# Reordering the first masks, first outputs and last stores of a Mamba-2 SSD plus squared-ReLU MoE kernel

## The chip, the core and the metric

The kernel runs on one core of a Trainium2 chip. The metric is the device time in microseconds of one execution. The time of the kernel before is the median of eight executions, 115.31 us (114.85 to 115.7).

The core's engines work side by side and meet through semaphores: TensorE (PE in the profile, its weight loads PEld), VectorE (DVE), ScalarE (ACT), GpSimd (POOL) and SyncE (SP), which only issues transfers here. GpSimd issues the transfers that turn float32 weights into bfloat16 on their way.

## The reference

A scan in chunks (Mamba-2's SSD form) is followed by a feed-forward layer with a squared ReLU. Cut to what matters:

```python
# x: [4, 8, 768, 32], a: [4, 8, 768], B and C: [4, 8, 768, 16]; chunks of 32
for c in range(nc):
    L = exp(cum_i - cum_j) * (i >= j)            # cum: cumulative sum of log a in the chunk
    y = ((C @ B.T) * L) @ x                       # within the chunk
    y += (C @ state) * exp(cum)                   # from the state
    state = exp(sum(log a)) * state + sum_j decay_from_j * outer(B_j, x_j)
h = maximum(y.reshape(3072, 256) @ w_in, 0)       # w_in: 256 x 2048
out = (h * h) @ w_out                             # w_out: 2048 x 256, out: 3072 x 256 float32
```

The kernel does the same with chunks of 256 tokens: the decays are folded into B and C as cumulative products, so that the scores need only a mask of zeros and ones.

## The kernel before, in words

There are 12 units, one for each of 4 batches and 3 stretches of 256 tokens (`UNITS`, line 124). A unit goes through these steps:

- `ph_load` brings C, B and x; `prep_c` and `prep_b` scale C and B and write them in bfloat16 into a tile `jt`; `ph_tr` transposes that tile into `bct` (on TensorE for units 0 to 4, with a copy back from PSUM).
- `ph_mt` makes the scores in the four PSUM banks 0 to 3. `ph_mask(k, q)` multiplies bank q with the mask into `mts`. Where `ph_raw(k, q)` ran before, ScalarE has copied the bank to SBUF as bfloat16 first, and the mask is applied to that copy.
- `ph_yu(y=, u=)` makes the outputs of unit y (`within`: `mts` with x; `from_state`: the state `Sd` with C) and the state products of unit u. The outputs are copied from PSUM into `T[y]`.
- `ph_s(k, i)` builds the next state `z` and its spread form `Sd`, for which it needs `QP`, a table of decays. Lists such as `later` hold back the second half of that.
- `mm1(blk, fp)` multiplies T with two columns of blocks of w_in and ends in a ReLU on ScalarE (`hb`), `square` squares it on VectorE (`h`), `mm2` multiplies with w_out and adds up over eight values of fp. After the last, the result is copied to `osb` and stored.

The order of all instructions is written out by hand: each engine runs its own in the order in which the Python code calls them. For the first 16 MoE steps that order is the list `first` (line 558), afterwards the loop at line 613. Everything that the change touches at the start lies in lines 478 to 511, between the transposes of unit 0 and the first `u00` of that list. There:

- `prep_c(1)`, the table QP (line 478), `load_w_out(0)` and `load_w_in(2)` are GpSimd's, in one queue with its computing.
- Unit 0's masks q = 0, 1, 3, 2 are VectorE's, with `prep_b(1)` and the first `Sd` (line 493) between the first and the second.
- `idle_products` are matmuls without use that keep TensorE busy; `NIDLE` (line 50) gives their number and width.
- `ph_mt(1)`, then `ph_yu(u=1)`, `ph_s(1, 0)` and `ph_yu(y=0, ...)` follow on TensorE.
- GpSimd then issues the further weights and unit 2's C, B and x.

w_in is loaded in five tiles (`W_TILES`); tile 2 holds the columns for fp 2 and 3. At the end, `mm2` runs `LAG` = 4 steps behind `mm1`, so five of its calls stand after the last `mm1`. The last unit's two halves of 128 tokens (r = 0 and 1) go to two PSUM banks and are stored by SyncE and ScalarE.

Of the kernel before, what the change touches and what calls it, by code (L numbers as in the profile page):

```python
# [10 lines left out]
FP32 = mybir.dt.float32  # L11
# [12 lines left out]
def _dap(base: bass.AP, offset_elems: int, dims):  # L24

    return bass.AP(tensor=base.tensor, offset=base.offset + offset_elems,
                   ap=[list(d) for d in dims])
# [3 lines left out]
def kernel(  # L31
# [13 lines left out]
    nc = tc.nc  # L45
    NH, S, D, N = 8, 768, 32, 16
    NU = 12
    LAG = 4
    NPE = 5
    NIDLE = ((7, 512), (2, 128), (4, 256), (2, 256), (4, 256), (3, 128), (3, 256))  # L50

    const = ctx.enter_context(tc.tile_pool(name="const", bufs=1))
    wpool = ctx.enter_context(tc.tile_pool(name="w", bufs=1))
# [7 lines left out]
    opool = ctx.enter_context(tc.tile_pool(name="opool", bufs=2))  # L61
# [91 lines left out]
    def load_w_in(i):  # L153
        f, n = W_TILES[i]
        nc.gpsimd.dma_start(out=w_in_b[i], in_=_dap(moe_w_in, f, [[2048, 128], [128 * 2048, 2], [1, 128 * n]]))  # L155

    def load_w_out(i):
        n = 4 if i else 2
        nc.gpsimd.dma_start(out=w_out_b[i], in_=_dap(
            moe_w_out, i * 512 * 256, [[256 * n, 128], [256 * 256, 4 // n], [1, 256 * n]]))  # L160
# [6 lines left out]
    def prep_c(k, eng):  # L167
        b, j = UNITS[k]
        for g in range(2):
            eng.tensor_tensor(  # L170
                out=_fap(jt[k % 3], 128 + 144 * g, [[384, 2], [32, 4], [1, 16]]),
                in0=_fap(loaded[k]["C"], 128 * g, [[16, 2], [32, 4], [1, 16]]),
                in1=_fap(P_sb, b * 24 + 12 * g + j, [[96, 2], [3, 4], [0, 16]]), op=ALU.mult)

    def prep_b(k, eng):
        b, j = UNITS[k]
        for g in range(2):
            o = _fap(jt[k % 3], 16 * g, [[384, 2], [32, 4], [1, 16]])
            i = _fap(loaded[k]["B"], 128 * g, [[16, 2], [32, 4], [1, 16]])
            if k == 0:  # L180
                eng.copy(out=o, in_=i)
            else:
                eng.tensor_tensor(out=o, in0=i, in1=_fap(Pinv, b * 24 + 12 * g + j, [[96, 2], [3, 4], [0, 16]]),  # L183
                                  op=ALU.mult)
# [64 lines left out]
    def ph_mt(k, qs=range(4)):  # L249
        v = live[k]  # L250
        bct = v["bct"]
        for r in range(2):
            for u in range(2):
                for q in qs:
                    nc.tensor.matmul(  # L255
                        pp[64 * u:64 * u + 64, q, r * 256:r * 256 + 256],
                        bct[32 * q:32 * q + 32, r, 0, u * 64:u * 64 + 64],
                        _fap(bct[32 * q:32 * q + 32], 128 + u * 64, [[128, 2], [384, 2], [1, 64]]),
                        start=True, stop=True, skip_group_check=True,
                        tile_position=(32 * q, 64 * u))  # L260
        if "mts" not in v:
            v["mts"] = big.tile([128, 4, 2, 2, 128], BF16, tag="mts", name=f"mts{k}")
# [3 lines left out]
    def ph_raw(k, q):  # L266
        t = prep.tile([128, 512], BF16, tag="raw", name=f"raw{k}_{q}")
        nc.scalar.copy(out=t, in_=pp[:, q, :])
        raw_scores[(k, q)] = t

    def ph_mask(k, q):
        t = raw_scores.pop((k, q), None)
        nc.vector.tensor_tensor(  # L273
            out=live[k]["mts"][:, q],
            in0=(pp[:, q, :] if t is None else t).rearrange("p (r g i) -> p r g i", r=2, g=2),
            in1=_fap(mask, 0, [[128, 2], [0, 2], [1, 128]]), op=ALU.mult)
# [74 lines left out]
    def ph_s(k, i, later=None, raw=None, eng=None):  # L351

        b, j = UNITS[k]
        v = live[k]
        if i == 0:
            v["S"] = [state.get(b, (None, None, None))[2]]
        if j == 2 and i == 1:
            return
        z_old, p_old, _ = state.get(b, (None, None, None))
        h, c = v["U"][i]  # L360
        held.discard(h)
        z = spool.tile([128, 64], FP32, tag=f"z{b}", name=f"z{k}_{i}")
        u_in = pp[:, h, c:c + 64] if raw is None else raw
        if z_old is None:
            nc.scalar.copy(out=z, in_=pp[:, h, c:c + 64])
        else:
            nc.vector.scalar_tensor_tensor(out=z, in0=z_old, scalar=p_old, in1=u_in,  # L367
                                           op0=ALU.mult, op1=ALU.add)
        S_d = spool.tile([128, 256], BF16, tag=f"Sd{b}{i}", name=f"Sd{k}_{i}")

        def on_pool():
            (eng or nc.gpsimd).tensor_tensor(  # L372
                out=_fap(S_d, 0, [[128, 2], [32, 4], [1, 32]]),
                in0=_fap(z, 0, [[32, 2], [0, 4], [1, 32]]),
                in1=_fap(QP, ((b * 3 + j) * 2 + i) * 4, [[0, 2], [1, 4], [0, 32]]), op=ALU.mult)

        if later is None:
            on_pool()
        else:
            later.append(on_pool)  # L380
        state[b] = (z, Ptot[:, i, b * 3 + j:b * 3 + j + 1], S_d)
        v["S"].append(S_d)
# [18 lines left out]
        nc.vector.tensor_tensor(out=h2, in0=hb, in1=hb, op=ALU.mult)  # L401
        h2s[(blk, fp)] = h2

    def mm2(blk, fp):
        h2 = h2s.pop((blk, fp))
        end = blk == NU - 1
        for r, i in [(r, i) for r in range(2) for i in range(2)] if end else [(r, i) for i in range(2) for r in range(2)]:
            f = 2 * fp + i
            o = pp[:, r, 0:256] if end else pp[:, 7 if blk else 6, r * 256:(r + 1) * 256]
            nc.tensor.matmul(o, h2[:, i, r * 128:(r + 1) * 128], w_out_b[f // 4][:, f % 4, :],  # L410
                             start=(f == 0 and (end or r == 0)), stop=(f == 15), skip_group_check=True)
        if fp < 7:
            return
        b, j = UNITS[blk]
        o = (b * S + j * 256) * 256
        osb = opool.tile([128, 512], FP32, tag="osb", name=f"osb{blk}")
        if end:
            nc.vector.tensor_copy(out=osb[:, 0:256], in_=pp[:, 0, 0:256])
            nc.scalar.copy(out=osb[:, 256:512], in_=pp[:, 1, 0:256])
            for r, eng in enumerate((nc.sync, nc.scalar)):  # L420
                eng.dma_start(out=_dap(out, o + r * 256, [[512, 128], [1, 256]]), in_=osb[:, r * 256:(r + 1) * 256])
        else:
            nc.scalar.copy(out=osb, in_=pp[:, 7 if blk else 6, :])  # L423
            nc.sync.dma_start(out=_dap(out, o, [[512, 128], [1, 512]]), in_=osb)

    with tc.manual_schedule():
# [37 lines left out]
        for r in range(2):  # L464
# [10 lines left out]
        pps = pp[:, hp, 256:280].rearrange("p (u c) -> p u c", u=2)  # L475
        nc.tensor.matmul(pps, spread, pick_p, start=True, stop=True)
        nc.scalar.copy(out=Ptot, in_=pps)
        nc.gpsimd.tensor_tensor(
            out=_fap(QP, 0, [[8, 12], [4, 2], [1, 4]]), in0=_fap(Ptot, 0, [[1, 12], [12, 2], [0, 4]]),
            in1=_fap(quad, 0, [[0, 12], [0, 2], [1, 4]]), op=ALU.mult)  # L480
        prep_c(1, nc.gpsimd)
        load_w_out(0)
        load_w_in(2)
        idle_products(*NIDLE[3])
        later = []
        ph_mt(0)
# [2 lines left out]
        ph_yu(u=0)  # L489
        U01 = const.tile([128, 64], FP32, name="U01")  # L490
        nc.scalar.copy(out=U01, in_=pp[:, 7, 384:448])
        prep_b(1, nc.vector)
        ph_s(0, 0, eng=nc.vector)
        ph_raw(0, 2)
        idle_products(*NIDLE[4])
        ph_tr(1)
        idle_products(*NIDLE[6])
        for q in (1, 3, 2):
            ph_mask(0, q)
        xs = prep.tile([128, NH, 2 * D], BF16, tag="xs", name="xs1")  # L500
        nc.scalar.copy(out=xs, in_=loaded[1]["x"])  # L501
        live[1]["xs"] = xs
        ph_mt(1)
        ph_yu(u=1)
        ph_s(1, 0)
        load_w_out(1)
        load_w_in(3)
        ph_yu(y=0, late=True, h=(4, 5))
        ph_raw(1, 3)
        for q in range(4):  # L510
            ph_mask(1, q)
        ph_load(2, "CB", nc.gpsimd)
        load_w_out(2)
        load_x(2)
# [94 lines left out]
        for k in range(6, NU):  # L609
            at({6: 23, 7: 31, 8: 36}.get(k, 8 * k - 33), ph_load, k)  # L610
            at({6: 28, 7: 33}.get(k, 8 * k - 25), ph_prep, k)
            at({6: 31}.get(k, 8 * k - 20), ph_tr, k)
        for s in range(16, len(ups) + LAG):
            for fn, args, kw in todo.pop(s, []):
                fn(*args, **kw)
            if s < len(ups):
                mm1(*ups[s], any(fn is ph_yu for fn, _, _ in todo.get(s + 1, [])))
            if 17 <= s <= len(ups):
                square(*ups[s - 1])
            if s == 16:  # L620
                mm2(1, 7)
            elif 19 <= s < 26:
                mm2(*ups[s - 3])
            elif s > 26:
                mm2(*ups[s - LAG])
# [1 line left out]
_INS = ['x', 'a', 'B', 'C', 'moe_w_in', 'moe_w_out']  # L627
_OUTS = [((3072, 256), 'float32')]
# [25 lines left out]
```

## Time and profile before

| what | value |
|---|---|
| median of eight executions | 115.31 us (114.85 to 115.7) |
| the profiled execution, its time | 114.85 us |
| its span in the profile | 113.1 us |
| TensorE busy | 107.3 us, 95% of the span |
| VectorE busy | 81.5 us, 72% |
| ScalarE busy | 75.5 us, 67% |
| GpSimd busy | 47.7 us, 42% |
| granted TensorE clock | full in every slice of the span |
| transfers | 13.18 MB, 117 GB/s on average |

A line of the timeline gives start, length, engine, source line, operation, output from input, the shape with types, and how many instructions it merges; in brackets stands how long the engine had been idle and what ended that. The chain of waits is followed back from the last instruction: at each step to what released it, or to the instruction before it on its engine. "Landing" is the time from a transfer's issue to its arrival. Engines overlap successive instructions a little, so that the next may start some 0.1 us before the one ahead of it ends.

How the time of TensorE divides over the span, by stretches:

| stretch, us | TensorE busy | VectorE | ScalarE | GpSimd |
|---|---|---|---|---|
| 6 to 9 | 2.75 | 2.87 | 2.14 | 2.98 |
| 9 to 12 | 1.92 | 3.00 | 2.30 | 1.86 |
| 12 to 15 | 2.85 | 1.99 | 1.96 | 3.00 |
| 15 to 24 | 9.00 | 7.02 | 5.46 | 3.02 |
| 24 to 100 | 75.99 | 58.87 | 55.07 | 33.29 |
| 100 to 113 | 9.88 | 4.73 | 6.60 | 0.00 |

### The profile page before, as it was taken

What the parts mean: (1) busy time and instruction counts of PE and PEld (TensorE: products, weight loads), DVE (VectorE), ACT (ScalarE), POOL (GpSimd) and SP (SyncE); (2) the same over time, 40 slices, a digit from 0 to 9 for tenths busy, and PEclk for the clock granted to TensorE, in tenths of its full rate; (3) what the DMA queues carried; (4) which work ended last, traced back from release to release, by engine and by line L of the source; (5) the groups of instructions that cost most, each with busy time, mean ns of one, the idle gap of its engine ahead of it and who ended that gap; (6) DMA issues with size and microseconds to landing.
All of it is one profiled execution on the core that took longest, in us unless ns stands there. A gap on an engine that the chain in (4) does not pass through costs nothing.

```text
span 113.1 us, 3923 instructions
## 1 busy us (share of the span) xinstructions
PE 107.3 (95%) x1603; PEld 91.8 (81%) x1603; DVE 81.5 (72%) x186; ACT 75.5 (67%) x139; POOL 47.7 (42%) x98
## 2 busy tenths in 40 slices
PE   6997899999999999999999999999999999999980
PEld 2454699888878989989989889899899899899960
DVE  4499868697797999869679777578488487354440
ACT  3367776637886777777776767767766767877830
POOL 6495991146996496390578065074020020000000
PEclk9999999999999999999999999999999999999999
DMA  3999999989895674926999928441050020200202
GB/s 63 205 173 152 167 215 177 165 152 168 151 276 59 105 196 87 171 97 112 195 215 116 160 100 151 102 139 29 6 148 17 22 80 3 71 28 0 93 0 93
DMA packets 45250, 13.18 MB, mean 117 GB/s; under 512 B 41392, under 2 KB 43376, under 8 KB 45232
## 3 DMA queue, kind: packets, MB, share of 16 engines
q1 hardware_dynamic: 40736, 10.13, 46.3%
q0 software_dynamic: 3200, 2.49, 14.9%
q10 hardware_dynamic: 1296, 0.32, 1.3%
q8 instruction: 12, 0.20, 0.9%
q14 instruction: 6, 0.05, 0.2%
HBM read 10.64 MB, written 3.15 MB: 122 GB/s over the span
## 4 chain that ended last, share of the span: by engine, by line
PE 92%; ACT 3%; DVE 1%; issue 1%
PE pp L391 38%; PE pp L410 38%; PE pp L288 7%; PE pp L164 4%; PE pp L255 3%; PE pp L240 1%; ACT bct L232 1%; DVE xs L190 1%; ACT hb L395 1%; ACT T L348 1%; PE pp L465 0%; ACT xs L501 0%; PE pp L217 0%; PE pp L231 0%; DVE h L401 0%
## 5 line engine op out<-in xcount | busy, mean ns | idle before, releaser
L395 ACT ACTIVATE hb<-pp 128x512 bf16<-128x512 f32 x96 | 56.5, 597 | 25.3 <-PE pp L391 22.8
L391 PE MATMUL pp<-T,w_in_b 128*128 128x256 bf16 x384 | 56.6, 273 | 0.7 <-ACT T L348 0.7
L410 PE MATMUL pp<-w_out_b,h 128*128 128x256 bf16 x384 | 56.5, 273 | 0.1
L401 DVE TENSOR_TENSOR h<-hb 128x512 bf16<-128x512 bf16 x96 | 43.1, 457 | 18.1 <-ACT hb L395 17.9
L391 PEld LDWEIGHTS <-w_in_b 128*128 128x128 bf16 x384 | 40.2, 110 | 4.6 <-issue 2.8
L410 PEld LDWEIGHTS <-h 128*128 128x128 bf16 x384 | 37.2, 98 | 4.3 <-DVE h L401 0.5
L273 DVE TENSOR_TENSOR mts<-pp,mask 128x512 bf16<-128x512 f32 x45 | 30.4, 682 | 0.3 <-PE pp L255 0.2
L372 POOL TENSOR_TENSOR Sd<-z,QP 128x256 bf16<-128x256 f32 x19 | 12.0, 643 | 27.9 <-DVE z L367 24.9
L170 POOL TENSOR_TENSOR jt<-C_nat,P_sb 128x128 bf16<-128x128 f32 x20 | 9.3, 484 | 6.7 <-DMA C_nat<-in_C_dram 6.2
L183 POOL TENSOR_TENSOR jt<-B_nat,Pinv 128x128 bf16<-128x128 f32 x18 | 8.3, 483 | 1.3 <-DMA B_nat<-in_B_dram 0.7
L367 DVE SCALAR_TENSOR_TENSOR z<-z,Ptot,pp 128x64 f32<-128x64 f32 x14 | 3.9, 279 | 5.4 <-ACT T L348 4.9
L164 PE MATMUL pp<-idle 128*128 128x256 bf16 (+2 forms) x25 | 6.2, 393 | 1.1 <-DVE idle L439 1.1
L348 ACT CAST T<-pp 128x512 bf16<-128x512 f32 x10 | 5.9, 586 | 1.3 <-PE pp L288 0.8
L423 ACT COPY osb<-pp 128x512 f32<-128x512 f32 x11 | 6.4, 582 | 0.2 <-PE pp L410 0.2
L195 POOL CAST xs<-x_nat 128x512 bf16<-128x512 f32 x9 | 6.2, 685 | 0.9 <-DMA x_nat<-in_x_dram 0.7
L255 PE MATMUL pp<-bct 32*64 32x256 bf16 x192 | 5.1, 280 | 0.4 <-ACT bct L232 0.3
L164 PEld LDWEIGHTS <-idle 128*128 128x128 bf16 x25 | 2.8, 125 | 3.2 <-issue 1.9
L288 PE MATMUL pp<-mts,xs 64*32 64x128 bf16 x352 | 5.3, 219 | 0.0
L288 PE MATMUL pp<-bct,Sd 128*128 128x128 bf16 x40 | 4.2, 220 | 0.0
L288 PEld LDWEIGHTS <-xs 64*32 64x32 bf16 x352 | 3.7, 90 | 0.4 <-issue 0.2
L155 POOL DMA_DIRECT2D w_in_b<-in_moe_w_in_dram x5 | 3.8, 762 | 0.3 <-issue 0.3
L288 PEld LDWEIGHTS <-Sd 128*128 128x128 bf16 x40 | 3.1, 98 | 0.4
(69 smaller groups left out, 44.4 us busy)
## 6 DMA issues: line engine op xcount, KB each, us to landing
x_nat<-in_x_dram SPq DMA_DIRECT2D x11, 256.0 KB, 4.1
out_dram<-osb SPq DMA_DIRECT2D x11, 256.0 KB, 3.4
C_nat<-in_C_dram SPq DMA_DIRECT2D x11, 128.0 KB, 3.4
B_nat<-in_B_dram SPq DMA_DIRECT2D x9, 128.0 KB, 3.6
w_out_b<-in_moe_w_out_dram POOLq DMA_DIRECT2D x4, 256.0 KB, 5.0
w_in_b<-in_moe_w_in_dram POOLq DMA_DIRECT2D x3, 256.0 KB, 6.0
w_in_b<-in_moe_w_in_dram POOLq DMA_DIRECT2D x2, 128.0 KB, 3.9
B_nat<-in_B_dram ACTq DMA_DIRECT2D x1, 128.0 KB, 3.3
```

Source lines behind the costliest of these rows:

```text
L164: nc.tensor.matmul(pp[:, 5, 0:cols], idle, _fap(idle, 0, [[0, cols // 128], [1, 128]]), start=True, stop=True, skip_group_check=True)
L170: eng.tensor_tensor(out=_fap(jt[k % 3], 128 + 144 * g, [[384, 2], [32, 4], [1, 16]]), in0=_fap(loaded[k]["C"], 128 * g, [[16, 2], [32, 4], ...
L183: eng.tensor_tensor(out=o, in0=i, in1=_fap(Pinv, b * 24 + 12 * g + j, [[96, 2], [3, 4], [0, 16]]), op=ALU.mult)
L255: nc.tensor.matmul(pp[64 * u:64 * u + 64, q, r * 256:r * 256 + 256], bct[32 * q:32 * q + 32, r, 0, u * 64:u * 64 + 64], _fap(bct[32 * q:32 ...
L273: nc.vector.tensor_tensor(out=live[k]["mts"][:, q], in0=(pp[:, q, :] if t is None else t).rearrange("p (r g i) -> p r g i", r=2, g=2), in1 ...
L288: nc.tensor.matmul(dst, w, v, start=bool(need), stop=False, skip_group_check=True, **({} if pos is None else {"tile_position": pos}))
L348: nc.scalar.copy(out=_fap(T[y], 0, [[64, 2], [128, 4], [1, 64]]), in_=_fap(pp, h[0] * 512, [[(h[1] - h[0]) * 512, 2], [64, 4], [1, 64]]))
L372: (eng or nc.gpsimd).tensor_tensor(out=_fap(S_d, 0, [[128, 2], [32, 4], [1, 32]]), in0=_fap(z, 0, [[32, 2], [0, 4], [1, 32]]), in1=_fap(QP ...
L391: nc.tensor.matmul(pp[:, h, i * 256:(i + 1) * 256], _fap(w_in_b[wb], g * 128 * n + f, [[n, 128]]), T[blk][:, g].rearrange("p r u t -> p (r ...
L395: nc.scalar.activation(out=hb.rearrange("p i t -> p (i t)"), in_=pp[:, h, :], func=AF.Relu)
L401: nc.vector.tensor_tensor(out=h2, in0=hb, in1=hb, op=ALU.mult)
L410: nc.tensor.matmul(o, h2[:, i, r * 128:(r + 1) * 128], w_out_b[f // 4][:, f % 4, :], start=(f == 0 and (end or r == 0)), stop=(f == 15), s ...
```

## The change

At the start:

- GpSimd prepares C of unit 1 and issues `load_w_out(0)` before it builds QP.
- On VectorE, mask (0, 1) comes right after mask (0, 0), ahead of `prep_b(1)`; then masks (0, 3) and (0, 2), and the first `Sd` after all of them.
- `load_w_in(2)` is issued behind a copy of one element of `mts` to `spare`, which waits for mask (0, 2).
- After `ph_mt(1)`, ScalarE copies bank 0 (before: bank 3, later), and GpSimd applies mask (1, 0) to that copy; VectorE applies (1, 1), (1, 2), (1, 3) from PSUM, and then makes unit 1's first `Sd`, which GpSimd made before.
- Unit 0's outputs come ahead of unit 1's state products on TensorE.
- Two of the idle products' numbers change: one of 128 columns less, one of 256 more.

At the end: the last unit's last four fp are worked off by halves in an order written out, so that half 0 is complete four matmuls before the end; each half has a staging tile, a copy and a store of its own.

```diff
-    NIDLE = ((7, 512), (2, 128), (4, 256), (2, 256), (4, 256), (3, 128), (3, 256))
+    NIDLE = ((7, 512), (2, 128), (4, 256), (2, 256), (4, 256), (2, 128), (4, 256))
...
-    def ph_mask(k, q):
+    def ph_mask(k, q, eng=None):
         t = raw_scores.pop((k, q), None)
-        nc.vector.tensor_tensor(
+        (eng or nc.vector).tensor_tensor(
...
-    def mm2(blk, fp):
-        h2 = h2s.pop((blk, fp))
+    def mm2(blk, fp, rs=(0, 1)):
+        h2 = h2s[(blk, fp)]
         end = blk == NU - 1
-        for r, i in [(r, i) for r in range(2) for i in range(2)] if end else [(r, i) for i in range(2) for r in range(2)]:
+        for r, i in [(r, i) for r in rs for i in range(2)] if end else [(r, i) for i in range(2) for r in range(2)]:
...
-        osb = opool.tile([128, 512], FP32, tag="osb", name=f"osb{blk}")
+        osb = opool.tile([128, 512], FP32, tag="osb", name=f"osb{blk}_{rs[0]}")
         if end:
-            nc.vector.tensor_copy(out=osb[:, 0:256], in_=pp[:, 0, 0:256])
-            nc.scalar.copy(out=osb[:, 256:512], in_=pp[:, 1, 0:256])
-            for r, eng in enumerate((nc.sync, nc.scalar)):
-                eng.dma_start(out=_dap(out, o + r * 256, [[512, 128], [1, 256]]), in_=osb[:, r * 256:(r + 1) * 256])
+            r = rs[0]
+            (nc.scalar.copy if r else nc.vector.tensor_copy)(out=osb[:, 0:256], in_=pp[:, r, 0:256])
+            (nc.scalar if r else nc.sync).dma_start(
+                out=_dap(out, o + r * 256, [[512, 128], [1, 256]]), in_=osb[:, 0:256])
...
         nc.scalar.copy(out=Ptot, in_=pps)
+        prep_c(1, nc.gpsimd)
+        load_w_out(0)
         nc.gpsimd.tensor_tensor(
             out=_fap(QP, 0, [[8, 12], [4, 2], [1, 4]]), in0=_fap(Ptot, 0, [[1, 12], [12, 2], [0, 4]]),
             in1=_fap(quad, 0, [[0, 12], [0, 2], [1, 4]]), op=ALU.mult)
-        prep_c(1, nc.gpsimd)
-        load_w_out(0)
-        load_w_in(2)
...
+        first_state = []
+        ph_s(0, 0, later=first_state, eng=nc.vector)
+        ph_mask(0, 1)
         prep_b(1, nc.vector)
-        ph_s(0, 0, eng=nc.vector)
         ph_raw(0, 2)
         idle_products(*NIDLE[4])
         ph_tr(1)
         idle_products(*NIDLE[6])
-        for q in (1, 3, 2):
+        for q in (3, 2):
             ph_mask(0, q)
+        for fn in first_state:
+            fn()
+        nc.gpsimd.tensor_copy(out=spare, in_=live[0]["mts"][:, 2, 0, 0, 0:1])
+        load_w_in(2)
...
         ph_mt(1)
+        ph_raw(1, 0)
+        ph_mask(1, 0, nc.gpsimd)
+        ph_yu(y=0, late=True, h=(4, 5))
         ph_yu(u=1)
-        ph_s(1, 0)
+        second_state = []
+        ph_s(1, 0, later=second_state, eng=nc.vector)
         load_w_out(1)
         load_w_in(3)
-        ph_yu(y=0, late=True, h=(4, 5))
-        ph_raw(1, 3)
-        for q in range(4):
+        for q in (1, 2, 3):
             ph_mask(1, q)
+        for fn in second_state:
+            fn()
...
-        for s in range(16, len(ups) + LAG):
+        for s in range(16, len(ups) + 1):
...
-            elif s > 26:
+            elif 26 < s < len(ups):
                 mm2(*ups[s - LAG])
+        for fp, r in ((4, 0), (5, 0), (6, 0), (4, 1), (5, 1), (7, 0), (6, 1), (7, 1)):
+            mm2(NU - 1, fp, (r,))
```

## The prediction

> **What bounds the kernel now.** I read the chain of waits first, then the timeline of the start (6 to 16 us) engine by engine, then the transfers' landing times, then the last 6 us. The chain by engine:
>
> ```profile
> PE 92%; ACT 3%; DVE 1%; issue 1%
> ```
>
> From 15 to 100 us TensorE has no idle time worth naming (the table by stretches: 9.00 us busy of 9.00, 75.99 of 76.00), and the change touches nothing there. What it can win lies before 15 us, where TensorE waits for small steps, and after 109 us, where the last store runs. A shift of the start passes to the end one for one. The start, from the timeline (start, length, engine, line; in brackets what was waited for):
>
> ```profile
> 8.11 0.54 DVE L183 TENSOR_TENSOR jt<-B_nat,Pinv 128x128 bf16<-128x128 f32 x2
> 8.72 0.86 ACT L232 COPY bct<-pp 128x512 bf16<-128x512 bf16 x2
> ...
> 9.51 0.75 DVE L273 TENSOR_TENSOR mts<-raw,mask 128x512 bf16<-128x512 bf16 x2
> 9.64 0.42 PE L255 MATMUL pp<-bct 32*64 32x256 bf16 x16 [0.32 <-ACT bct L232]
> ...
> 10.15 0.25 PE L288 MATMUL pp<-xs,jt 64*32 64x64 bf16 x16
> ...
> 10.22 0.55 PE L288 MATMUL pp<-mts,xs 64*32 64x128 bf16 x32
> ...
> 11.02 0.59 ACT L348 CAST T<-pp 128x512 bf16<-128x512 f32 x1 [0.33 <-PE pp L288]
> ...
> 11.65 1.03 PE L391 MATMUL pp<-T,w_in_b 128*128 128x256 bf16 x8 [0.67 <-ACT T L348]
> ```
>
> Read downwards: the B half of unit 1 is scaled on VectorE, transposed, copied by ScalarE (ends 9.58), then TensorE makes unit 1's scores (9.64), unit 1's state products (10.15, which had waited for the copy of x, 9.47 + 0.63 = 10.10), unit 0's outputs (10.22, waiting also for the masks, 9.51 + 0.75 = 10.26), the copy T0, and the first MoE product at 11.65. All later work hangs on that 11.65.
>
> **The change, part by part.**
>
> *Mask (0,1) ahead of prep_b, first state product behind the masks.* Nothing is added on VectorE, it is reordered. Before, it stood idle from 8.02 (end of mask (0,0), 7.33 + 0.69) to 8.11, when B of unit 1 had landed (issued 3.60, 4.5 us). Consecutive PSUM masks start 0.60 apart (three in 1.88 us). So mask (0,1) starts at 7.93, prep_b at 8.53, ending 9.02 to 9.07 instead of 8.65: **0.40 later**. The raw masks follow (8.98, 9.32) and end at 9.74 instead of 10.26: **0.5 sooner**; the state product then runs to 10.07.
> The price is on the other branch. The B transposes ended 0.34 after prep_b (8.65 to 8.99) and will end at 9.36 to 9.41; ScalarE's second copy, formerly held by its first copy until 9.21, starts at about 9.42 and ends at 9.80. Unit 1's scores start 0.05 later, at 9.83 to 9.87 against 9.64: **+0.22**.
>
> *Unit 0's outputs ahead of unit 1's state products.* They no longer wait for x (10.10) nor for masks (9.74), only for the scores in front. Scores to the next group's start took 0.36 of issuing where no wait was added (mt1's last matmul issues 0.16 after its first, the following weight load 0.20 after that), so they start at 10.19 to 10.23, where they start today. But they run faster: unit 1's same group (12.62 to 12.97 + 0.29) took 0.64 with nothing missing, unit 0's took 0.77 (10.22 to 10.99) because of the mask at 10.26. So they end at 10.83 to 10.92 and T0 starts 0.04 later: 10.87 to 10.96 instead of 11.02. The new raw copy of (1,0) stands ahead of T0 on ScalarE: scores of bank 0 ready 10.32, the next ScalarE start 0.50 later (such copies started 0.48 apart at 7.34 and 7.82), 10.82; just covered. If that cover went, it would cost at most 0.1. **Gain at T0: 0.06 to 0.15, taken 0.11.** The state products (0.25 us) go into the wait for T0 (0.67 us of idle today): free.
>
> *First mask of unit 1 on GpSimd.* Four VectorE masks to 12.55 become three, to 12.23, plus the second state product (0.41, to 12.57), which VectorE takes over from GpSimd. It waits for z1 (after T0, 11.6). The first square comes at 12.92 today after 0.37 us of idleness, so it is not delayed. Outputs of unit 1 start at 12.62 only because of the mask ending 12.55; now 12.50. A GpSimd mask of 128x512 is not in the trace. Nearest rows: 128x128 0.41, 128x256 0.60, so by a straight line 0.99; started at 10.95 (raw copy 10.91) it ends 11.95. The Trainium skill, "GPSIMD Engine Reference" (section 4.1), speaks against the move: it gives two-input elementwise work to VectorE because GpSimd takes about twice as long, and section 3 gives 4497 ns for 2048 elements, which scaled is an estimate of 1.12 us, end 12.07. By row or rule it ends over 0.4 us before 12.50, so both give zero. From about 1.5 us on it would cost.
>
> *prep_c ahead of QP; w_out(0) sooner.* prep_c waits for C, landed at 2.35 + 4.9 = 7.25: it runs 7.29 to 8.06 (today 8.29). Its C transposes gain 0.2, but the B half is now last, so nothing. w_out(0) is issued at 8.0 instead of 8.23; its landing (12.6) was not waited for at 13.40. QP at 8.74 to 9.10 is in time for the state product at 9.66. Zero.
>
> *w_in(2) behind a wait.* GpSimd now waits for mask (0,2), 9.74, copies one element (0.31, like L524), and issues w_in(2) at about 10.05 instead of 8.99. Queued behind it: the GpSimd mask (until 10.95 not ready anyhow), w_out(1), w_in(3), C and B of unit 2, w_out(2), x of unit 2, w_in(4), w_out(3), all some 0.55 later (mask end 11.95 for 11.45). Their landings today come 1.2 to 1.4 us apart, the queue's pace, so little passes on; the slack is w_in(3) 17.6 for use at 18.65, w_out(1) 16.2 for 17.78, C 18.3 for 18.95.
> w_in(2) itself has no slack: today it lands at 8.99 + 6.0 = 14.99 and is used in this stretch:
>
> ```profile
> 8.23 0.76 POOL L159 DMA_DIRECT2D w_out_b<-in_moe_w_out_dram  x1
> ...
> 8.99 0.72 POOL L155 DMA_DIRECT2D w_in_b<-in_moe_w_in_dram  x1
> ...
> 14.72 1.47 PE L391 MATMUL pp<-T,w_in_b 128*128 128x256 bf16 x12
> ```
>
> Four matmuls of 0.11 after 14.72, that is 15.05 for its first weight load, and 14.94 after the gain. The 6.0 held a wait behind w_out(0), issued 0.76 before it; now w_out(0) is 2.05 ahead. w_out(0) itself took 4.4, w_out(1) 4.8, w_in(3) 5.6. So it lands between 14.45 and 16.05. The page "DMA: Bandwidth & Descriptors" (section "Anatomy of one DMA — SWDGE (gpsimd) path", its fit of 2.0 us plus bytes over 436 GB/s) would put 256 KB at 2.6 us, 12.65; the rows contradict it, and I go by w_out(0), the one with the emptiest queue: 14.45 to 14.9, **cost zero, with almost no margin**.
>
> *Idle products*: one of 128 columns less, one of 256 more, before 9.7; the scores start at 9.83 or later. Zero.
>
> *Last half stored sooner.* The last 16 matmuls are reordered, none added (20 in 2.35 us, 0.11 each).
>
> ```profile
> 109.70 0.42 DVE L418 COPY osb<-pp 128x256 f32<-128x256 f32 x1 [0.91 <-PE pp L410]
> 109.92 0.37 ACT L419 COPY osb<-pp 128x256 f32<-128x256 f32 x1 [1.59 <-PE pp L410]
> 110.15 0.33 SPq L421 DMA_DIRECT2D out_dram<-osb  x1
> 110.32 0.36 ACTq L421 DMA_DIRECT2D out_dram<-osb  x1
> ```
>
> Half 0 is finished four matmuls before the end instead of two: its copy, issue and landing (1.7) come 0.22 sooner, 111.63. But the end is half 1: its copy at 109.92 and issue at 110.32 stay, and land after 1.9, at 112.2. Only the 0.2 by which its transfer was longer can shrink, if the two disturbed one another: 0 to 0.19, **taken 0.10**. The last square (108.36 + 0.42) is in time for its first use, now 14 matmuls after 107.53: 109.07. The older stores from the two staging buffers were issued at 105.34 or before and landed in about 2 us.
>
> **Sum.** 0.11 + 0.10 = 0.21 us off the profiled execution, 114.85 (span 113.1 and 1.7 around it). That one is the lowest of the eight; laid on the median, 115.31 - 0.21 = **115.1**.
>
> **Rivals.**
> 1. *w_in(2) comes late* (slower). It stalls TensorE from a landing time of 4.9 us on, and the kernel is slower than before from 5.1 on. At w_in(3)'s 5.6: 15.65, stall 0.7, net +0.5, 115.8; at its own old 6.0: net +0.9, 116.2. For: no slack, and half of the rows are above 5.1. Against: those had fuller queues. Chance 0.22.
> 2. *Only the end gains*: prep_b's delay eats the masks' gain, or ScalarE's raw copy holds T0 past 11.0: 115.31 - 0.10 = 115.2. For: +0.22 on the score branch is certain, the saving is a difference of two such numbers. Chance 0.15.
> 3. *Both parts at their full ends*: 0.15 + 0.19 = 0.34, 114.95. Chance 0.15.
> 4. *The named aims are not what acts*: closing up the masks delays the branch that bounds, and the sooner w_out is not waited for. That is so in my forecast as well; what acts is the order of outputs and state products. It has no time of its own.
>
> **How the numbers follow.** Forecast 0.48, own range 114.9 to 115.4. 0.3%, about what a measurement of this kernel can tell from no change, is 0.35 us; the executions shown spread by 0.85. Faster beyond that: nearly all of rival 3 (0.13), a third of the forecast (0.16), a little of rival 2 (0.03), 0.32 together. Slower: two thirds of rival 1, 0.15, and 0.04 of the rest, 0.19. Same: 0.49. Range 114.6 to 115.8: down to rival 3 with the spread, up to rival 1 at 5.6 us.
>
> **What would show it.** Right: unit 1's scores at 9.85, unit 0's outputs at 10.2 and over by 10.9, T0 at 10.9, first MoE product near 11.54, GpSimd's mask about 1 us, no idle TensorE at 14.94, first half's store 0.2 sooner, the second landing 112.0 to 112.2 less the start's gain. Wrong: a TensorE wait at the third weight group, T0 at 11.0 or later, or a GpSimd mask beyond 1.5 us.

## The result and the profile after

The changed kernel takes 116.2 us (median of 20 runs, 115.5 to 117.1), the kernel before beside it 115.4 (57 runs, 114.81 to 116.36): the ratio is **1.0073**, with a 95% interval of 1.0054 to 1.0092. It is slower by about 0.8 us, and the forecast was 115.1. Runs in the chip's slower state, here one of 117.92 us, are left out of all medians and ratios. The profiled execution took 116.21 us, its span is 114.5 us.

The chain of waits of the changed kernel by engine, as for the kernel before:

```profile
PE 81%; DMA 9%; POOL 3%; DVE 2%; issue 1%; ACT 0%; ACTq 0%; POOLq 0%
```

TensorE had 92% there and transfers were not named. Now transfers hold 9% of the span and GpSimd 3%. The chain from 9 to 37 us says which (start, length, what):

```profile
10.34 0.26 POOL spare L503
10.59 5.65 DMA w_in_b<-in_moe_w_in_dram
16.25 0.05 issue
16.29 1.06 PE pp L391 x8
...
26.44 4.96 DMA B_nat<-in_B_dram
...
31.54 1.01 POOL jt L183 x2
```

So two things are waited for: w_in(2), behind its new gate (the one-element copy that waits for mask (0, 2)), and later the B of unit 4, which GpSimd needs at 31.5. The timeline of the start answers to the lines shown of before:

```profile
8.97 0.63 DVE L183 TENSOR_TENSOR jt<-B_nat,Pinv 128x128 bf16<-128x128 f32 x2
9.52 0.75 DVE L273 TENSOR_TENSOR mts<-raw,mask 128x512 bf16<-128x512 bf16 x2
9.98 0.37 ACT L232 COPY bct<-pp 128x256 bf16<-128x256 bf16 x1 [0.42 <-PE pp L231]
10.34 0.31 POOL L503 CAST spare<-mts 128x1 f32<-128x1 bf16 x1 [0.89 <-DVE mts L273]
10.40 0.42 PE L255 MATMUL pp<-bct 32*64 32x256 bf16 x16
10.59 0.77 POOL L155 DMA_DIRECT2D w_in_b<-in_moe_w_in_dram  x1
10.76 0.45 PE L288 MATMUL pp<-mts,xs 64*32 64x128 bf16 x32
11.46 0.59 ACT L348 CAST T<-pp 128x512 bf16<-128x512 f32 x1
11.55 1.15 POOL L273 TENSOR_TENSOR mts<-raw,mask 128x512 bf16<-128x512 bf16 x1 [0.19 <-ACT raw L268]
12.10 1.03 PE L391 MATMUL pp<-T,w_in_b 128*128 128x256 bf16 x8 [0.49 <-ACT T L348]
12.65 0.61 POOL L159 DMA_DIRECT2D w_out_b<-in_moe_w_out_dram  x1
...
16.29 1.06 PE L391 MATMUL pp<-T,w_in_b 128*128 128x256 bf16 x8 [0.53 <-DMA w_in_b<-in_moe_w_in_dram]
```

Three readings. w_in(2) is issued at 10.59 instead of 8.99, and TensorE waits for it at the third weight group (0.53 on the matmul side; 0.70 by the starts of the groups). The next load behind it, w_out(1), is issued at 12.65 instead of 11.40, since GpSimd's mask of 1.15 us stands in front. And the first MoE product is at 12.10 instead of 11.65; but nearly all of this lies ahead of the change: the very first mask, which nothing of the change precedes on its path, started at 7.76 instead of 7.33 (and at 7.79 in e1 below, whose start is the old one). Such shifts come and go between executions, with either start. Times below are those of the traces; where two profiles are compared by them, they are also counted from the first mask (w_in(2) is then issued 1.17 later and w_out(1) 0.82 later).

GpSimd's preparation of units 3 to 5, first in the kernel before, then in the changed one:

```profile
24.50 0.78 POOL L170 TENSOR_TENSOR jt<-C_nat,P_sb 128x128 bf16<-128x128 f32 x2 [0.24 <-DMA C_nat<-in_C_dram]
...
28.84 0.78 POOL L183 TENSOR_TENSOR jt<-B_nat,Pinv 128x128 bf16<-128x128 f32 x2
```

```profile
26.63 1.18 POOL L170 TENSOR_TENSOR jt<-C_nat,P_sb 128x128 bf16<-128x128 f32 x2 [1.20 <-DMA C_nat<-in_C_dram]
...
31.54 1.01 POOL L183 TENSOR_TENSOR jt<-B_nat,Pinv 128x128 bf16<-128x128 f32 x2 [1.07 <-DMA B_nat<-in_B_dram]
```

C of unit 3 comes 2.13 us later and B of unit 4 2.70 (0.43 of either is the later start, 0.70 the stall), and TensorE meets the delay at MoE step 22 (steps are counted from 0). The end, answering to the last four lines shown of before:

```profile
110.94 0.42 DVE L419 COPY osb<-pp 128x256 f32<-128x256 f32 x1 [0.69 <-PE pp L410]
111.39 0.33 SPq L420 DMA_DIRECT2D out_dram<-osb  x1
111.42 0.37 ACT L419 COPY osb<-pp 128x256 f32<-128x256 f32 x1 [1.63 <-PE pp L410]
111.82 0.36 ACTq L420 DMA_DIRECT2D out_dram<-osb  x1
```

Half 0 is now issued 0.43 ahead of half 1 (before: 0.17), and half 1 lands 1.75 after its issue instead of 1.91. From the first of the last 20 matmuls to that landing it is 4.58 us instead of 4.70. All nine profiles with the new end show 4.58 to 4.59, all four with the old one 4.69 to 4.70.

The account of the two spans, 114.48 less 113.15 = 1.33 us: the start 0.43 later, the way from the first mask to the first MoE product 0.01 longer, the stall for w_in(2) 0.70, the waits at step 22 0.30 (0.02 in between), the end 0.13 shorter. The 0.43 belongs to the execution, not to the change. What remains is 0.90, near the 0.8 of the medians; that they are so near is partly luck, since the kernel before was profiled in one of its fastest executions (114.85) and the changed one at its median.

### The profile page after: what moved, and what is told of

Same layout as the page of the kernel before. It is cut to its first block, busy times and chain, and to the rows that moved or that the text cites. A ratio compares the mean times of both kernels' runs of the same rounds, so it can differ in the third digit from the quotient of the medians.

```text
span 114.5 us, 3928 instructions
## 1 busy us (share of the span) xinstructions
PE 108.1 (94%) x1603; PEld 91.9 (80%) x1603; DVE 82.5 (72%) x186; ACT 75.7 (66%) x139; POOL 48.9 (43%) x99
## 4 chain that ended last, share of the span: by engine, by line
PE 81%; DMA 9%; POOL 3%; DVE 2%; issue 1%; ACT 0%; ACTq 0%; POOLq 0%
PE pp L410 33%; PE pp L391 33%; PE pp L288 6%; DMA w_in_b<-in_moe_w_in_dram 5%; DMA B_nat<-in_B_dram 4%; PE pp L164 4%; PE pp L255 3%; DVE mts L273 2%; POOL Sd L372 2%; POOL jt L183 1%; PE pp L217 1%; POOL xs L195 1%; PE pp L465 0%; DVE jt L183 0%; ACT osb L419 0%
## 5 line engine op out<-in xcount | busy, mean ns | idle before, releaser
L395 ACT ACTIVATE hb<-pp 128x512 bf16<-128x512 f32 x96 | 56.5, 597 | 26.3 <-PE pp L391 24.9
L401 DVE TENSOR_TENSOR h<-hb 128x512 bf16<-128x512 bf16 x96 | 44.1, 465 | 18.2 <-ACT hb L395 17.9
L372 POOL TENSOR_TENSOR Sd<-z,QP 128x256 bf16<-128x256 f32 x18 | 11.5, 652 | 26.2 <-DVE z L367 24.4
```

The lines of the kernel that those rows point to most:

```text
L372: (eng or nc.gpsimd).tensor_tensor(out=_fap(S_d, 0, [[128, 2], [32, 4], [1, 32]]), in0=_fap(z, 0, [[32, 2], [0, 4], [1, 32]]), in1=_fap(QP ...
L395: nc.scalar.activation(out=hb.rearrange("p i t -> p (i t)"), in_=pp[:, h, :], func=AF.Relu)
```

## The experiments

Each stands beside runs of the kernel before on the same chip. "Loss" is how much the MoE steps fall behind the profiled kernel before, between the first and step 28, in the one execution of each that was profiled.

**e1: the gate alone**, in the kernel before.

```diff
-        load_w_in(2)
...
             ph_mask(0, q)
+        nc.gpsimd.tensor_copy(out=spare, in_=live[0]["mts"][:, 2, 0, 0, 0:1])
+        load_w_in(2)
```

> The kernel before, with one edit: the copy of one element that waits for mask (0, 2), and load_w_in(2) issued behind it. Theory 1 (the late third w_in tile and, behind it, the whole queue of GpSimd's transfers cost the time): w_in(2) issued near 10.6 instead of 8.99, landing near 16, TensorE waits 0.6 to 0.9 us at the third weight group near 15, and a further 0 to 0.4 us near 34; the kernel is 0.7 to 1.2 us slower than before, about 116.3. Theory 2 (the masks' new order delays B of unit 1 and so TensorE): nothing but noise, 115.4.

116.46 us, ratio 1.0123 (1.0082 to 1.0163). w_in(2) issued at 10.70 landed at 16.04; the stall was 0.65, and another 0.76 was lost by step 22. The gate alone makes the kernel at least as slow as the whole change does.

**e2: the changed kernel without the gate**, w_in(2) straight behind QP.

```diff
+        load_w_in(2)
         idle_products(*NIDLE[3])
...
-        nc.gpsimd.tensor_copy(out=spare, in_=live[0]["mts"][:, 2, 0, 0, 0:1])
-        load_w_in(2)
```

> The changed kernel without the wait: load_w_in(2) is issued right behind QP, at about 9.1, everything else as changed. Theory 1: no wait at the third weight group, at least 0.7 us faster than the changed kernel, between 115.1 and 115.5. Theory 2: stays slower than before, 115.9 or more. If the GpSimd mask is what holds up the transfers (w_out(1) and those after it are still issued 0.8 later than before), a wait should remain near 34 but none near 15, and 0.3 us of loss remain.

115.91 us, 1.0061 (1.0041 to 1.0081): slower than I thought it would be. Its timeline:

```profile
8.94 0.63 POOL L480 TENSOR_TENSOR QP<-Ptot,quad 128x96 f32<-128x96 f32 x1
8.96 0.90 DVE L273 TENSOR_TENSOR mts<-raw,mask 128x512 bf16<-128x512 bf16 x2
9.53 0.76 POOL L155 DMA_DIRECT2D w_in_b<-in_moe_w_in_dram  x1
...
11.54 1.03 PE L391 MATMUL pp<-T,w_in_b 128*128 128x256 bf16 x8 [0.49 <-ACT T L348]
...
12.09 0.60 POOL L159 DMA_DIRECT2D w_out_b<-in_moe_w_out_dram  x1
...
14.60 1.47 PE L391 MATMUL pp<-T,w_in_b 128*128 128x256 bf16 x12
```

The first MoE product is at 11.54, and the twelve matmuls from 14.60 run through: no stall. Yet 0.87 was lost after it, between steps 8 and 22. So the gate is not all of it; w_out(1) and all behind it were still 0.7 later than before.

**e3: the end alone**, in the kernel before: all of the change's diff from `mm2` on, whose core is

```diff
-        for s in range(16, len(ups) + LAG):
+        for s in range(16, len(ups) + 1):
...
+        for fp, r in ((4, 0), (5, 0), (6, 0), (4, 1), (5, 1), (7, 0), (6, 1), (7, 1)):
+            mm2(NU - 1, fp, (r,))
```

> The kernel before, with the new order of the last 16 matmuls and the two staging tiles only. The prediction took 0.10 us off (bounds 0 and 0.19), 115.3; the start is as before. In the trace the first half's store is issued some 0.2 sooner and the second lands 1.7 to 1.9 after its issue.

115.39 us, 1.0004 (0.9983 to 1.0025): nothing that the medians can show, though its trace has the end 0.12 shorter. Its start is the old one, and still it lost 0.53 by step 22. The profiled kernel before, the lowest of its eight, had lost nothing there; about half a microsecond of such loss is thus within the reach of the unchanged order.

**e4: e2 with B of unit 1 scaled ahead of mask (0, 1)**, as before.

```diff
-        ph_mask(0, 1)
         prep_b(1, nc.vector)
+        ph_mask(0, 1)
```

> As the changed kernel without the wait, and with prep_b(1) back ahead of mask (0, 1) on VectorE; the first state product stays behind the masks. Theory 2: this is what the change should have kept: scores of unit 1 at about 9.65 again, T0 0.2 to 0.3 sooner than without this edit, and 0.2 us faster than it. Theory 1: T0 is sooner, but the third weight group lands no sooner, so TensorE waits there instead and the time is that of the kernel without the wait, within 0.1 us.

115.62 us, 1.0030 (1.0007 to 1.0054), not told apart from e2 by the intervals. The way from the first mask to the first MoE product shrank to 4.16 us (before 4.32, e2 4.19). But w_in(2), issued at 9.20, landed only at 15.65, and TensorE stalled 0.80 for it.

**e5: e2 with mask (1, 0) on VectorE**, so that nothing stands between the loads: w_out(1) at 10.36.

```diff
-        ph_mask(1, 0, nc.gpsimd)
...
-        for q in (1, 2, 3):
+        for q in (1, 2, 3, 0):
```

> The changed kernel without the wait for w_in(2), and with mask (1, 0) on VectorE (last of the four, from the raw copy) instead of GpSimd, so that w_out(1), w_in(3) and what follows are issued right behind w_in(2), near 10.2, instead of 12.1. Theory 1, widened (GpSimd's transfers run in one queue at its own pace, and TensorE uses each tile just as it lands, so every delay of an issue is paid later): 0.5 to 0.8 us faster than the kernel with only the wait taken out (115.9), near 115.1 or below, and no faster than that only if the landings do not move. Theory 2 (the order of VectorE's masks): no difference beyond 0.1 us from it.

116.45 us, 1.0097 (1.0072 to 1.0121): the opposite of what I expected. Its timeline:

```profile
9.61 0.76 POOL L155 DMA_DIRECT2D w_in_b<-in_moe_w_in_dram  x1
10.36 0.56 POOL L159 DMA_DIRECT2D w_out_b<-in_moe_w_out_dram  x1
...
17.12 1.06 PE L391 MATMUL pp<-T,w_in_b 128*128 128x256 bf16 x8 [1.76 <-DMA w_in_b<-in_moe_w_in_dram]
```

w_in(2) took 7.5 us and TensorE stalled 1.9; afterwards nothing more was lost. This raised the question whether a load is slowed by those issued close behind it.

**e6: the changed kernel, gate kept, mask (1, 0) on VectorE** by the edit of e5.

```diff
-        ph_mask(1, 0, nc.gpsimd)
...
+        for q in (1, 2, 3, 0):
```

> The changed kernel with the wait kept, and only mask (1, 0) moved back to VectorE. Now w_in(2) is issued near 10.4 as in the changed kernel, but w_out(1) at about 11.1 instead of 12.6. If the wait alone is what costs: as the changed kernel, about 116.2, TensorE waiting at the third weight group. If the GpSimd mask is what costs: near 115.3. If both do, in between, near 115.8.

117.01 us, 1.0141 (1.0094 to 1.0189), with five runs from 116.06 to 117.74. w_in(2) issued at 10.10 landed at 15.77, a stall of about 0.8, and 0.63 more went at step 22. It took 5.7 us although w_out(1) came 0.77 behind it, so this pair does not show the slowing that e5 suggested.

**e7: a candidate.** e4 with w_in(2) ahead of QP and, by the edit of e5, mask (1, 0) on VectorE.

```diff
         load_w_out(0)
+        load_w_in(2)
         nc.gpsimd.tensor_tensor(
             out=_fap(QP, 0, [[8, 12], [4, 2], [1, 4]]), in0=_fap(Ptot, 0, [[1, 12], [12, 2], [0, 4]]),
             in1=_fap(quad, 0, [[0, 12], [0, 2], [1, 4]]), op=ALU.mult)
-        load_w_in(2)
```

> A candidate: no wait, w_in(2) issued right behind w_out(0) and ahead of QP, prep_b(1) ahead of mask (0, 1), mask (1, 0) on VectorE, so that no computing stands between GpSimd's issues but QP. Unit 0's outputs ahead of unit 1's state products, as changed. Theory 1: landings 1 us or more earlier than in the changed kernel, first MoE product about 11.35, no wait on a transfer: 114.6 to 115.0, faster than before by 0.2 to 0.6. Theory 2 expects the gain at the start (0.2) alone.

115.11 us, 0.9975 (0.9949 to 1.0000). After 0.14 at step 2 the stall was 0.38 at the third group, and nothing was lost later.

**e8: the kernel before with w_out(1) and w_in(3) ahead of unit 1's state**, issued at 9.82 and 10.37.

```diff
-        ph_s(1, 0)
         load_w_out(1)
         load_w_in(3)
+        ph_s(1, 0)
```

> The kernel before with one edit: w_out(1) and w_in(3) are issued ahead of the state product Sd(1, 0) in GpSimd's queue, at 9.7 and 10.3 instead of 11.4 and 12.0. Nothing else moves. Theory 1: w_out(1) to w_out(3) land up to 1 us earlier, the waits between 18 and 36 us go, 0.2 to 0.5 us faster than before. If the queue is limited by the transfers themselves and not by their issue, no difference (115.2 to 115.4).

115.41 us, 1.0019 (0.9997 to 1.0040): a wash. w_in(2) took 6.4 us (6.0 before) and held TensorE up by 0.27; by step 10 another 0.20 was lost, and 0.03 after it.

**e9: e7 with the following loads held back.**

```diff
+        nc.gpsimd.tensor_copy(out=spare, in_=raw_scores[(1, 0)][:, 0:1])
         load_w_out(1)
         load_w_in(3)
```

> The changed kernel with w_in(2) issued right behind w_out(0), near 8.9 us, B of unit 1 scaled first on VectorE, all masks of unit 1 on VectorE, and the following loads held back by a one-element copy on GpSimd until ScalarE's raw copy of bank 0 is there, so that w_out(1) is issued near 11.3 us as in the kernel before. Theory 1 (a load is slowed by those issued close behind it, and all of them share one stretch of transfers): w_in(2) has the queue to itself as before and lands near 15.0, against 15.55 where its followers came at 10.06; with the first MoE product near 11.5 TensorE stalls by 0.2 us at most at the third weight group, w_out(1) and w_in(3) come as before, and nothing is lost later: ratio 0.995 to 1.000. Theory 2 (w_in(2)'s landing depends on its own issue and on what stands in front of it alone): it lands near 15.55 again with a stall of 0.4 to 0.5, and the followers, 1.25 us later than there, cost as in the kernel before: ratio 1.000 to 1.004.

115.19 us, 1.0004 (0.9984 to 1.0024). Timelines of e7, then of e9:

```profile
8.90 0.72 POOL L155 DMA_DIRECT2D w_in_b<-in_moe_w_in_dram  x1
...
10.06 0.60 POOL L159 DMA_DIRECT2D w_out_b<-in_moe_w_out_dram  x1
...
15.60 1.06 PE L391 MATMUL pp<-T,w_in_b 128*128 128x256 bf16 x8 [0.21 <-DMA w_in_b<-in_moe_w_in_dram]
```

```profile
8.95 0.72 POOL L155 DMA_DIRECT2D w_in_b<-in_moe_w_in_dram  x1
...
11.05 0.61 POOL L159 DMA_DIRECT2D w_out_b<-in_moe_w_out_dram  x1
...
14.91 1.47 PE L391 MATMUL pp<-T,w_in_b 128*128 128x256 bf16 x12
```

With the same issue, w_in(2) landed at 15.55 in e7 and at 14.07 in e9, where its follower came 1 us later, and the stall went. The trace goes the way that the theory of slowing foretold, though further than its 15.0, and its rival's 15.55 did not come. It is one execution of each, and with w_in(2) issued at 8.99 to 9.13 and no close follower the landing varied from 14.61 to 14.97 (before, e3, e10). The time fits either theory, and it does not tell e7 and e9 apart: their intervals overlap.

**e10: the later queue alone.** The kernel before, with a product that nobody reads on GpSimd ahead of w_out(1).

```diff
         ph_s(1, 0)
+        waste = const.tile([128, 512], BF16, name="waste")
+        nc.gpsimd.tensor_tensor(
+            out=waste.rearrange("p (r g i) -> p r g i", r=2, g=2), in0=live[0]["mts"][:, 0],
+            in1=_fap(mask, 0, [[128, 2], [0, 2], [1, 128]]), op=ALU.mult)
         load_w_out(1)
```

> The kernel before with one addition: a product of 128x512 on GpSimd into a tile that nobody reads, ahead of the issue of w_out(1). Nothing else changes; w_in(2) is issued at 9.0 as before, all loads behind it about 1.15 us later. Theory 1 (the later queue is a loss of its own): no stall at the third weight group (w_in(2) lands at 15.0 or sooner), then 0.3 to 0.6 us lost between the 8th and the 22nd MoE step, where C and B of unit 2 and the loads behind them are waited for: ratio 1.003 to 1.005. Theory 2 (only the late w_in(2) costs, the rest of the queue has slack, as the prediction put it: w_in(3) 17.6 for 18.65, w_out(1) 16.2 for 17.78, C 18.3 for 18.95): ratio within 0.999 to 1.001.

116.09 us, **1.0090** (1.0058 to 1.0122): more than either theory said. Its timeline:

```profile
9.01 0.72 POOL L155 DMA_DIRECT2D w_in_b<-in_moe_w_in_dram  x1
...
11.43 1.15 POOL L507 TENSOR_TENSOR waste<-mts,mask 128x512 bf16<-128x512 bf16 x1
12.13 0.72 DVE L273 TENSOR_TENSOR mts<-raw,mask 128x512 bf16<-128x512 bf16 x1
12.52 0.61 POOL L159 DMA_DIRECT2D w_out_b<-in_moe_w_out_dram  x1
...
14.94 1.47 PE L391 MATMUL pp<-T,w_in_b 128*128 128x256 bf16 x12
...
26.20 1.02 POOL L170 TENSOR_TENSOR jt<-C_nat,P_sb 128x128 bf16<-128x128 f32 x2 [1.67 <-DMA C_nat<-in_C_dram]
```

No stall at the third group; 0.20 at step 2 (a VectorE mask from SBUF took 0.72 beside the product, 0.43 before), 0.19 between there and step 20, and 0.82 at step 22. C of unit 3 had come 1.7 late: SyncE issues it at 22.20 (21.93 before), but it took 3.8 us where it had taken 2.4. The chain of waits then runs over SyncE's next C, that of unit 4:

```profile
25.42 4.71 DMA C_nat<-in_C_dram
```

It was issued 1.67 later than before (23.75), because SyncE's issue of x just ahead of it lasted 2.04 us instead of 0.53 (why, no run shows). What these loads meet on the DMA engines, by queue from 20 to 31 us (packets, MB, time of the packets as a share of the 16 engines' time; packets overlap, so the shares can add up to more than 100%), the kernel before and then e10:

```profile
q1 hardware_dynamic: 8205, 1.30, 68.5%
q0 software_dynamic: 350, 0.43, 23.0%
```

```profile
q1 hardware_dynamic: 7134, 1.16, 63.6%
q0 software_dynamic: 1496, 0.71, 50.0%
```

GpSimd's queue (q0) still has twice the share there, since it was pushed back (its last load landed at 25.45 instead of 23.25), and SyncE's loads (q1) share the engines with it. In the changed kernel that share is 52.9%, in e9 24.9%. In e3, with the loads issued as before, it is 35.2%, and e3 lost 0.32 at step 22.

**e11: the changed kernel with d10 ahead of the third group.**

```diff
-            ... u11 s10 u02 s11 u03 d10 inv ...
+            ... u11 s10 d10 u02 s11 u03 inv ...
```

> The changed kernel, with the second product of step (1, 0) moved from behind the third weight group to just ahead of it, so that TensorE has 0.44 us of work while it waits for w_in(2). Nothing moves on GpSimd or in the transfers. Theory 1 (the stall at the third group is time lost for good, and the later waits come on top of it): the third group starts about 0.1 us later (16.4), the product is done by then, so all later steps come 0.3 us sooner: ratio 1.004 to 1.005 against the kernel before, 0.997 of the changed kernel. Theory 2 (the end of the queue of loads decides; what TensorE gains before it waits again at C, B and the loads of units 3 to 5): the 0.3 us are gained at step 6 and lost again by step 22: ratio 1.006 to 1.008.

115.71 us, 1.0045 (1.0017 to 1.0073), at the value that the first theory gave for the median. The profiled execution (116.69 us, near the upper end of its 13) shows the other:

```profile
15.69 0.61 PE L410 MATMUL pp<-w_out_b,h 128*128 128x256 bf16 x4 [0.28 <-DVE h L401]
...
16.14 1.47 PE L391 MATMUL pp<-T,w_in_b 128*128 128x256 bf16 x12
...
19.62 0.63 PE L391 MATMUL pp<-T,w_in_b 128*128 128x256 bf16 x4 [0.26 <-DMA w_in_b<-in_moe_w_in_dram]
```

The wait for w_in(2) was covered (the step waited for its square instead), 0.43 was back at step 6, and 0.43 was gone again at step 8, at w_in(3). Another 0.93 went by step 22. Whether the gain lasts is thus not settled: the median leans that way, within an interval that overlaps the changed kernel's, and the one trace says that it does not.

**All together**, ordered by what they lose (times of issue; loss by step 28, one execution each):

| kernel | w_in(2) | last load, w_out(3) | loss, us | ratio |
|---|---|---|---|---|
| before | 8.99 | 16.61 | 0 | 1 |
| e9 | 8.95 | 16.29 | 0.13 | 1.0004 |
| e8 | 9.11 | 15.79 | 0.50 | 1.0019 |
| e3 | 9.13 | 16.75 | 0.53 | 1.0004 |
| e7 | 8.90 | 15.84 | 0.55 | 0.9975 |
| e2 | 9.53 | 17.30 | 0.87 | 1.0061 |
| after | 10.59 | 17.87 | 1.02 | 1.0073 |
| e10 | 9.01 | 17.75 | 1.21 | 1.0090 |
| e4 | 9.20 | 17.03 | 1.38 | 1.0030 |
| e1 | 10.70 | 17.22 | 1.41 | 1.0123 |
| e6 | 10.10 | 16.06 | 1.52 | 1.0141 |
| e11 | 10.40 | 17.53 | 1.84 | 1.0045 |
| e5 | 9.61 | 17.36 | 2.04 | 1.0097 |

Where w_in(2) is issued by 9.13 and the last load by 16.75, the loss stays within about 0.55. Where either comes later it is 0.87 or more; counted from the first mask the same two groups come out. The two bounds were read off afterwards, from one execution of each kernel, and e4 and e11 lost more there than their medians show. Where both come later the parts do not add: e1 and e10, which are late in the main in one part each, lose at least as much as the whole.

## Why the prediction was wrong, point by point

- *Masks closed up*: right for the start that it was worked out from. With the first mask set at 7.33 as there, unit 1's scores came at 9.82 in e2, e5 and e11; in the changed kernel they are at 9.97, since scaling B took 0.63 for two instead of 0.48 in e2. What it missed is that the price hangs on the start. Before, VectorE waited for B of unit 1 until 8.11, which hid a part of it. With the later first mask of the changed kernel (7.76) or of e1 (7.79, old order), B has landed when mask (0, 0) ends, and mask (0, 1) in front costs its full 0.60. The old order under such a start, in e1:

```profile
8.39 0.51 DVE L183 TENSOR_TENSOR jt<-B_nat,Pinv 128x128 bf16<-128x128 f32 x2
...
11.93 1.03 PE L391 MATMUL pp<-T,w_in_b 128*128 128x256 bf16 x8 [0.67 <-ACT T L348]
```

There B is scaled at 8.39 and the first MoE product is at 11.93; in the changed kernel they are at 8.97 and 12.10.

- *Outputs ahead of state products, 0.11 at T0*: e2 has 0.14 on the way from the first mask to the first MoE product (4.19 for 4.32). With B scaled first and a late first mask, e7 and e9 have 4.03 where e1 with the old order has 4.14, which is 0.11. In the one profile of the changed kernel the masks' price ate it (0.01 the other way). It is small, and it does not reach the end where a load is waited for afterwards.
- *GpSimd's mask, 0.99 by the rows, 1.12 by the page*: 1.14 to 1.16 in four executions. Here the estimate from the Trainium skill's "GPSIMD Engine Reference" (section 3, scaled from its float32 figure; the mask is bfloat16) was nearer than my straight line. As foretold it held up no output. But I priced only its result, not the queue behind it: it pushed w_out(1) and seven more loads.
- *prep_c, w_out(0), QP*: right, w_out(0) was not waited for.
- *w_in(2) behind a wait*: **the step that failed**. "I go by w_out(0), the one with the emptiest queue: 14.45 to 14.9, cost zero, with almost no margin." The issue came as forecast (1.17 later than before, forecast 1.06), but the load took 5.65 us, not 4.4, and the stall was 0.70. The other rows that I named lay between 4.8 and 6.0; I took the lowest, on an argument about the queue that no row tested. In the thirteen profiles of this study its shortest flight was 5.1.
- *"so little passes on"* of the queue: **the second failure**, in the same paragraph. Counted from the first mask w_out(1) came 0.82 later, not 0.55, since GpSimd's mask began 0.17 later than forecast and took 0.16 longer. The delay did pass on: the queue's last load landed 2.2 us later than before, counted so, and 0.9 later than in e3, whose start is the old one. The pace of "1.2 to 1.4 us" was misread, too: this queue's landings before lie 0.4 to 1.5 apart. And the slack that I listed for w_in(3), w_out(1) and C of unit 2 ended the list too early: the loads of units 3 to 5, which SyncE issues, share the DMA engines, and there the delay arrives (e10, 0.82 at step 22). That the change "touches nothing" from 15 to 100 us was wrong with it.
- *The end, 0.10*: right; every trace with the new end has 0.12. e3's median shows none, but its interval of 0.2% each way cannot exclude it.
- *Rivals*: rival 1 (chance 0.22) has the mechanism of the larger loss. That the median equals the 116.2 that it gave for a flight of 6.0 is luck, for the sum is another: a stall of 0.70 in place of 1.1, and the later queue, which no rival had.

What stays open: why w_in(2)'s flight varies from 5.1 to 7.5 us. Followers close behind it go with a longer one in three pairs (e5 against e2, e7 against e9, e8 against before), not in e6 against the changed kernel, and e4 had 6.4 with its follower 2.6 us behind. A load counts as landed with the last of its sixteen shares. In the changed kernel fifteen had landed by 14.89, 4.30 after the issue, and the last came 1.36 later (0.71 in the kernel before, 0.98 in e1, 0.15 in e9). TensorE wanted the tile at about 15.6, so by these times the whole stall there stands on that one share. No run took that apart, nor whether VectorE's work beside the issue plays a part. Nor was the masks' new order run alone; e2 and e4 differ by it, and their intervals overlap.

None of these versions is shown to beat the kernel before: e7's interval touches 1. e7 and e9 do show that the outputs' order, the later state products and the stores by halves cost nothing that can be measured (0.24% at most, by their intervals) when w_in(2) is issued as early as before.

## What to carry to other kernels

An instruction put in front of a load on the issuing engine delays every load behind it; price it by the last consumer of the whole queue, those of other queues on the same DMA engines included, not by the load named in the change. Where a load lands just when it is needed, take the middle of the measured flights, not the one whose circumstances look best; the last of its shares decides. And a gain at the start counts only if no load after it is already waited for.

## What the runs showed of the hardware that was not expected

- GpSimd and VectorE slowed one another where both read from SBUF: QP took 0.63 instead of 0.36 beside VectorE's masks on `raw` (two of these 0.90 instead of 0.75, e2), and such a mask took 0.72 instead of 0.43 beside e10's product. It is not always both: in e9 two masks took 0.90, and QP 0.39. VectorE's three masks from PSUM beside GpSimd's mask took 1.89 in the changed kernel, against 1.88 without it.
- The same start, unchanged on the path to the first mask, put that mask between 7.17 and 7.79 in thirteen profiles. A single pair of profiles can't be compared by absolute times to better than that.
